# A recurrent attention block and a squared-ReLU FFN: inverting the first round in blocks of 32 steps, later rounds four batches at once, with GpSimd issuing its own loads

## The chip, the cores and the metric

The kernel runs on one core of a Trainium2 chip. The metric is the time of one execution in device microseconds. The core has five engines with an instruction stream each: TensorE (PE in the profile, its weight loads PEld), VectorE (DVE), ScalarE (ACT), GpSimd (POOL) and SyncE (SP), which here only issues transfers. Each engine takes its instructions in the order of the program and waits where data are not there yet.

## The reference

Inputs are r, k, v, w, a, b of shape (4 batches, 8 heads, 768 steps, 40), and the FFN weights w_in (320 x 2048) and w_out (2048 x 320). Each batch and head has a 40 x 40 state:

```
for t in range(S):
    y[t]  = r[t] @ state
    Sa    = state @ a[t]
    state = state * w[t][None, :] - outer(Sa, b[t]) + outer(v[t], k[t])
x   = y rearranged to (B*S, H*D) = (3072, 320)
out = maximum(x @ w_in, 0)**2 @ w_out
```

## The kernel before

The 768 steps are cut into 6 chunks of 128. `order` lists 24 items, chunk by chunk and within a chunk batch by batch: item i has chunk `c = i // 4` and batch `bb = i % 4`. Within a chunk the recurrence becomes matrix products and the inverse of a triangular 128 x 128 matrix per head. That matrix is treated as two diagonal halves of 64 steps (`HC`) and the block N between them.

What is done for an item:

- `early(i)`, wrapped in `prepare(i)`, which first issues the loads of w, b and a for item i + 1 (`load_early`, L133): transposes, running products of the decays and their reciprocals on VectorE (L303 to L312), the 128 x 128 product per head on TensorE, its copy on ScalarE (L319). The triangular parts go to DRAM in `kept_d`, the block N in `kept_n`, decays in `kept_e`. For items 0 and 1 decays and N stay in SBUF. `store` puts each store in `line`, and `tick` issues it on SP's queue a step or two later.
- `solve(u, eng)`, on GpSimd for a unit of items: it loads the triangular halves from `kept_d` into `half_n` (loads issued by SP, L346), and in 63 steps of a product (L352) and a subtraction (L354) makes the inverses in `half_t`, which GpSimd stores to `kept_t` (L356). Units: two batches at once in chunks 0 and 1, four batches in chunks 2 to 5, 8 units in all.
- `inverses(i, g)`: at the first item of a unit it writes out the next unit's solve, then loads item i's N and T (L375, SP).
- `rest(i)`: products with k, r, v and their masks; at its end or in its middle it calls `inverses`.
- `chain(i)`: the dependent part. It needs T and N (L458 to L467; L459 is ScalarE's first copy behind a T product), updates the state and writes the item's tokens.
- `ffn()`: one generator over 12 groups of two items. A group has 24 steps: 16 of w_in products with ReLU and square, and 8 of w_out products.
- `weights(n)`: the weights come as 64-bit floats and are turned into 32-bit ones by five VectorE and two ScalarE instructions per piece (L220 to L230): 12 wide pieces of w_in (512 columns), 16 narrow ones of w_out (320 columns).

The order of the work is written out by hand. `weave` merges several generators step by step into one program order. The head prepares items 0 and 1, solves unit 0, prepares items 2 and 3, does `rest` for items 0 and 1 and rounds 16 pieces beside them. Then for each item i a weave of 12 steps (`TOTAL`) has chain(i), rest(i + 1), one or two prepares, and as many FFN steps as `share` says: (steps in the weave, steps ahead of it), where the steps ahead cover the wait for an inverse. Items 0 to 3 prepare two items each (4 to 11), later ones item i + 8.

All matrix products go through the helper at L78 and all stores of `store` through L99, so these lines appear for many operations; the tile names tell them apart.

Of the kernel before, what the change touches and what calls it, by code (L numbers as in the profile page):

```python
# [8 lines left out]
FP32 = mybir.dt.float32  # L9
I32 = mybir.dt.int32  # L10
U32 = mybir.dt.uint32
Alu = mybir.AluOpType
# [5 lines left out]
def kernel(  # L18
# [22 lines left out]
    nc = tc.nc  # L41
    ctx.enter_context(tc.manual_schedule())
    B, H, S, D = r.shape
    DM = H * D
# [6 lines left out]
    DP = 64  # L51
    NF = DFF // 128
    GB = 2
    LEAD = 2 * B


    NT = NP - 1
# [25 lines left out]
    def new(name, shape, bufs):  # L83
        return work.tile(shape, FP32, tag=name, name=name, bufs=bufs)
# [4 lines left out]
    def later(fn, steps=2):  # L89
        line.append([steps, fn])  # L90

    def tick():
        for entry in line:
            entry[0] -= 1
        while line and line[0][0] <= 0:
            line.pop(0)[1]()

    def store(out_, in_, steps=2):
        later(lambda: nc.sync.dma_start(out=out_, in_=in_), steps)  # L99

    quads = lambda t_: t_.rearrange("p (q t) -> p q t", q=NP)
    by_head = lambda t_: t_[:, :DM].rearrange("t (h d) -> t h d", h=H)
# [20 lines left out]
    def more_rings():  # L123
        for nm in ("k", "b", "r", "v"):
            rings[nm] = Ring(f"in_{nm}", 2, [128, H, DP], 0.0, pads)
# [32 lines left out]
        nc.gpsimd.memset(same[e * DP:(e + 1) * DP, :, e:e + 1], 1.0)  # L158

    more_rings()  # L160
    whole = lambda t_: t_

    UP, DOWN, A_ = range(3)
# [15 lines left out]
    room = w_out.rearrange("p f c -> p (f c)")  # L179
    wide_raws = [room[:, 2 * WI * i:2 * WI * (i + 1)] for i in range(4)]  # L180
    hidden = single("hid", [128, NF + 1, GB * C])
    RAWS = (NF + 1) * GB * C // (2 * DM)
    raws = [hidden.rearrange("p f t -> p (f t)")[:, 2 * DM * i:2 * DM * (i + 1)] for i in range(RAWS)]
    for raw in wide_raws:
        nc.gpsimd.memset(raw, 0.0)
    lowest = single("lowest", [128, 1])
# [13 lines left out]
    def fetch_weights():  # L200
        while count[0] < len(pieces):
            n = count[0]
            wide = n < NARROW
            if len(fetched) + len(begun) >= (4 if wide else RAWS):
                return
            dst, srcs = pieces[n]
            raw = wide_raws[n % 4] if wide else raws[n % RAWS]
            for row, m_, src in srcs:
                nc.scalar.dma_start(out=raw.bitcast(I32)[row:row + m_], in_=src.bitcast(I32))
            fetched.append((dst, raw))  # L210
            count[0] += 1
# [21 lines left out]
    def weights(n, pool=ps_f):  # L233
        for _ in range(n):
# [8 lines left out]
            else:  # L243
# [11 lines left out]

    kept_n = [dram.tile([HC, H, HC], FP32, tag=f"n{i}", name=f"kept_n{i}") for i in range(len(order))]
    Q = HC // 2
    kept_d = [[dram.tile([B, 2, H, Q, HC - n * Q], FP32, tag=f"d{c}{n}", name=f"kept_d{c}{n}") for n in range(2)]
              for c in range(NCH)]
    kept_e = [dram.tile([128, 3, NP, C + 2], FP32, tag=f"e{i}", name=f"kept_e{i}") for i in range(len(order))]  # L260

    units = [(c, b0, 2) for c in range(2) for b0 in range(0, B, 2)] + [(c, 0, B) for c in range(2, NCH)]
    unit_of = {c * B + b0 + n: u for u, (c, b0, nb) in enumerate(units) for n in range(nb)}
    columns = lambda nb: 128 // (nb * 2 * H)
    kept_t = [dram.tile([columns(nb), nb, 2, H, HC // columns(nb), HC], FP32, tag=f"t{u}", name=f"kept_t{u}")
              for u, (_, _, nb) in enumerate(units)]

    def turn(x_):
        p_ = psum(ps_w)
# [19 lines left out]
        return res  # L289

    turned = lambda nm, bufs: new(nm, [128, NP, 128], bufs)

    def early(i, g=None):

# [22 lines left out]
        t_ = new("N", [128, H, C], 1)  # L317
        for e, p_ in enumerate(products(bT, aT[:, :, :C])):
            nc.scalar.copy(t_[:, e * NP:(e + 1) * NP], p_)  # L319
        for n in range(2):  # L320
            for half in range(2):
                at = half * HC + n * Q
                store(kept_d[c][n][bb, half].rearrange("h s t -> s h t"), t_[at:at + Q, :, at:(half + 1) * HC], 1)
        if g is None:
            store(kept_n[i], t_[:HC, :, HC:], 1)
        else:
            g["dec"], g["N"] = dec, new("N21", [HC, H, HC], 2)
            nc.scalar.copy(g["N"], t_[:HC, :, HC:])
        yield

    def solve(u, eng):
        c, b0, nb = units[u]
        cols = columns(nb)
        rows, deep = 128 // cols, HC // cols

        ns = [new("half_n0", [128, Q, HC], 1), new("half_n1", [128, Q, Q], 1)]
        ts = new("half_t", [128, Q, HC], 1)[:, :deep]
        eng.memset(ts, 0.0)  # L340
        flat = ts.rearrange("p j t -> p (j t)")
        for col in range(cols):
            eng.memset(flat[col * rows:(col + 1) * rows, col::HC + cols], -1.0)
        for part, kept in zip(ns, kept_d[c]):
            for col in range(cols):
                nc.sync.dma_start(out=part[col * rows:(col + 1) * rows].rearrange("p s t -> p (s t)"),  # L346
                                  in_=kept[b0:b0 + nb].rearrange("b f h s t -> (b f h) (s t)"))
        yield
        for s in range(HC - 1):
            n, m_ = s // cols + 1, HC - 1 - s  # L350
            p_ = new("half_p", [128, 528], 1)[:, :n * m_].rearrange("p (j t) -> p j t", j=n)
            eng.tensor_tensor(p_, ns[s // Q][:, s % Q, s % Q + 1:].unsqueeze(1).to_broadcast([128, n, m_]),  # L352
                              ts[:, :n, s:s + 1].to_broadcast([128, n, m_]), Alu.mult)
            eng.tensor_tensor(ts[:, :n, s + 1:], ts[:, :n, s + 1:], p_, Alu.subtract)  # L354
            yield
        nc.gpsimd.dma_start(out=kept_t[u].rearrange("two b f h j t -> (two b f h) (j t)"), in_=flat)  # L356
        yield

    def inverses(i, g):
        bb, c = order[i]
        u = unit_of[i]
        if unit_of.get(i - 1) != u and u + 1 < len(units):
            for _ in solve(u + 1, nc.gpsimd):
                pass
        cols, b0 = columns(units[u][2]), units[u][1]
        g["T"] = new("T", [128, H, HC], 2)
        if "N" not in g:  # L370
            g["N"] = new("N21", [HC, H, HC], 2)
            nc.sync.dma_start(out=g["N"], in_=kept_n[i])
        for half in range(2):
            for col in range(cols):
                nc.sync.dma_start(out=g["T"][half * HC + col:(half + 1) * HC:cols],  # L375
                                  in_=kept_t[u][col, bb - b0, half].rearrange("h j t -> j h t"))

    def rest(i, g):
        bb, c = order[i]
# [14 lines left out]
        nc.vector.tensor_tensor(kT, kT_, down[:, :, 1:C + 1], Alu.mult)  # L394
        nc.vector.tensor_copy(ends, down[:, :, 0])
        if unit_of[i - 1 if i else i] == unit_of[i] and i > 1:
            inverses(i, g)
        yield
        g["A"] = masked("A", 4, kT, aT)
        yield  # L400
# [29 lines left out]
            nc.scalar.copy(sd.rearrange("p q e d -> p q (e d)"), quads(p_))  # L430
        yield
        if unit_of[i - 1 if i else i] != unit_of[i]:
            inverses(i, g)
        yield


# [110 lines left out]
    def run(gen):  # L547
        for _ in gen:
            tick()
# [11 lines left out]
            run(gen)  # L561

    def prepare(i, g=None):
        if 1 < i + 1 < len(order) and i + 1 not in early_loaded:
            load_early(i + 1)
        yield from early(i, g)

# [8 lines left out]
    def firsts(begin, end):  # L576
        gens = [prepare(i, ready.get(i)) for i in range(begin, end)]
        next(gens[0]), next(gens[0])
        for i, now in enumerate(gens):
            then = gens[i + 1] if i + 1 < len(gens) else iter(())  # L580
            next(now)
            next(then, None)
            tick()
            yield
            next(now)
            next(then, None)
            tick()
            yield
            run(now)
            yield  # L590

    run(firsts(0, 2))
    while line:
        tick()
    for _ in solve(0, nc.gpsimd):
        pass
    load(0)
    load(1)
    if moe_w_in.dtype != FP32:
        fetch_weights()  # L600

    def head():
        yield from firsts(2, 4)
        yield from rest(0, ready[0])
        yield from rest(1, ready[1])

    WITH = NARROW + 4
    weave((head(), 6 + 2 * 9, 0, WITH + 4), (weights(WITH, ps_c), WITH, 4, WITH + 6))
    while begun:
        rounded_second()  # L610
    while line:
        tick()
    tc.no_sync_barrier()
    inverses(0, ready[0])
    inverses(1, ready[1])
    TOTAL = STEPS // GB

    share = {0: (0, 0), 1: (0, 0), 2: (6, 10), 3: (8, 0), 4: (8, 8), 5: (8, 0)}
    rounding = weights(NF)
    for i in range(len(order)):  # L620
        bb, c = order[i]
        n, ahead = share.get(i, (TOTAL, 0))
        for _ in range(ahead):
            next(second)
            tick()
        tc.no_sync_barrier()
        parts = [(chain(i, ready.pop(i)), 9, 0, TOTAL)]
        if 1 < i + 1 < len(order):
            load(i + 1)
            ready[i + 1] = {}  # L630
            parts.append((rest(i + 1, ready[i + 1]), 9, 2, TOTAL))
        if i < B:
            parts += [(prepare(B + 2 * i), 5, 0, TOTAL - 5), (prepare(B + 2 * i + 1), 5, 5, TOTAL)]
        elif i + LEAD < len(order):
            parts.append((prepare(i + LEAD), 5, 0, TOTAL - 2))
        if i < 2:
            parts.append((some(rounding, 8 - 4 * i), 8 - 4 * i, 0, TOTAL))
        parts.append((some(second, n), n, 0, TOTAL))
        weave(*parts)
    while line:  # L640
        tick()
    run(second)
    while line:
        tick()


# [27 lines left out]
```

## Time and profile before

| what | value |
|---|---|
| three timed runs | 1188.52, 1174.78, 1188.54 us (median 1188.52) |
| the profiled execution: its time / its span | 1178.83 / 1177.1 us |
| mean granted TensorE clock | 0.917 |
| busy: PE / PEld / DVE / ACT / POOL | 999.4 / 829.6 / 491.1 / 233.5 / 731.4 us |
| the two groups of a solve, 504 instructions each (L352, L354) | 333.6 and 366.1 us |
| FFN products: w_in / w_out (matmul time) | 293.1 / 221.0 us |
| ScalarE's L459 copy of items 0, 1, 4, 8, 23 starts at | 131.75, 175.15, 321.9, 525.5, 1107.0 us |

The profile gives one execution. Lines of groups have the source line, engine, operation and tiles, then busy time, the mean time of one in ns, and idle time before it with its cause. Lines of waits give who waited for whom: total, times, longest. Lines of the chain and of timelines begin with the start and the duration in us. Lines of stretches give busy time and count for PE, PEld, DVE, ACT and POOL, then the granted clock (1.00 is full), the share of DMA, and GB/s. Busy time of a matmul includes its pipelined end.

### The profile page before, as it was taken

What the parts mean: (1) busy time and instruction counts of PE and PEld (TensorE: products, weight loads), DVE (VectorE), ACT (ScalarE), POOL (GpSimd) and SP (SyncE); (2) the same over time, 40 slices, a digit from 0 to 9 for tenths busy, and PEclk for the clock granted to TensorE, in tenths of its full rate; (3) what the DMA queues carried; (4) which work ended last, traced back from release to release, by engine and by line L of the source; (5) the groups of instructions that cost most, each with busy time, mean ns of one, the idle gap of its engine ahead of it and who ended that gap; (6) DMA issues with size and microseconds to landing.
All of it is one profiled execution on the core that took longest, in us unless ns stands there. A gap on an engine that the chain in (4) does not pass through costs nothing.

```text
span 1177.1 us, 18561 instructions
## 1 busy us (share of the span) xinstructions
PE 999.4 (85%) x7248; PEld 829.6 (70%) x7248; DVE 491.1 (42%) x1008; ACT 233.5 (20%) x511; POOL 731.4 (62%) x1085
## 2 busy tenths in 40 slices
PE   4232477889999899429999989999989999999998
PEld 3121466778788687318888878788778887888886
DVE  6289576354354155005525424544233242322211
ACT  1033121211221122002112112122122121221211
POOL 4687886488488699979997059994089990000000
PEclk9997556879989899859999989999999999999999
DMA  7946645747655934244663394354353421433000
GB/s 113 169 135 182 137 110 125 146 104 160 152 99 101 170 70 86 48 94 98 109 105 101 86 155 78 87 113 101 92 90 66 77 52 51 76 64 76 3 13 12
DMA packets 261992, 114.95 MB, mean 98 GB/s; under 512 B 243472, under 2 KB 248464, under 8 KB 260368
## 3 DMA queue, kind: packets, MB, share of 16 engines
q1 hardware_dynamic: 256704, 96.98, 43.3%
q10 hardware_dynamic: 4048, 10.49, 3.1%
q0 software_dynamic: 1152, 6.29, 1.4%
q8 instruction: 57, 0.93, 0.4%
q14 instruction: 31, 0.25, 0.1%
HBM read 77.34 MB, written 35.40 MB: 96 GB/s over the span
## 4 chain that ended last, share of the span: by engine, by line
PE 61%; POOL 9%; DVE 5%; DMA 4%; SPq 2%; issue 1%; ACT 0%; POOLq 0%; DVEq 0%; ACTq 0%
PE ps_f L78 34%; PE ps_c L78 16%; PE ps_w L78 6%; POOL half_t L354 5%; POOL half_p L352 4%; PE ps_w L271 4%; DMA dec<-kept_e 2%; DMA T<-kept_t 1%; SPq L133 1%; PE ps_c L428 1%; SPq L99 1%; PE ps_c L471 1%; DVE RV L287 1%; PE ps_w L418 1%; DMA half_n<-kept_d 1%
## 5 line engine op out<-in xcount | busy, mean ns | idle before, releaser
L352 POOL TENSOR_TENSOR half_p<-half_n,half_t 128x252 f32<-128x252 f32 (+52 forms) x504 | 333.6, 662 | 169.6 <-DMA half_n<-kept_d 130.6
L354 POOL TENSOR_TENSOR half_t<-half_t,half_p 128x252 f32<-128x252 f32 (+52 forms) x504 | 366.1, 726 | 39.5
L78 PE MATMUL ps_f<-tokens,w_in 128*128 128x256 f32 x1152 | 293.1, 399 | 0.0
L523 DVE TENSOR_TENSOR hid<-ps_f,hid 128x256 f32<-128x256 f32 x192 | 80.8, 421 | 412.9 <-ACT hid L522 412.8
L78 PEld LDWEIGHTS ps_f<-tokens,w_in 128*128 128x128 f32 x1152 | 216.0, 198 | 31.2 <-issue 0.4
L78 PE MATMUL ps_f<-w_out,hid 128*128 128x320 f32 x768 | 221.0, 437 | 0.0
L78 PEld LDWEIGHTS ps_f<-w_out,hid 128*128 128x128 f32 x768 | 140.7, 190 | 53.9 <-issue 0.2
L522 ACT ACTIVATE hid<-ps_f 128x256 f32<-128x256 f32 x192 | 73.8, 384 | 244.9 <-PE ps_f L78 244.9
L78 PE MATMUL ps_c<-xr,T 64*64 64x40 f32 x768 | 59.4, 239 | 54.1 <-DMA T<-kept_t 52.7
L78 PEld LDWEIGHTS ps_c<-xr,T 64*64 64x64 f32 x768 | 53.7, 147 | 70.3 <-issue 68.2
L78 PEld LDWEIGHTS ps_c<-in_v,A 128*128 128x128 f32 x384 | 50.5, 206 | 17.1 <-DVE w_out L230 14.7
L78 PE MATMUL ps_c<-in_v,A 128*128 128x40 f32 x384 | 49.1, 290 | 14.3 <-DVE w_out L230 14.3
L78 PE MATMUL ps_w<-dec,kvT 40*128 40x128 f32 x384 | 32.4, 316 | 27.3 <-DVE kvT L394 27.2
L78 PEld LDWEIGHTS ps_w<-dec,kvT 40*128 40x128 f32 x384 | 27.3, 215 | 32.2 <-DVE kvT L394 29.2
L78 PE MATMUL ps_w<-decay,bT 40*128 40x128 f32 x352 | 36.8, 340 | 15.4 <-DVE decay L312 13.8
L319 ACT COPY N<-ps_w 128x512 f32<-128x512 f32 x48 | 25.8, 589 | 119.6 <-PE ps_w L78 71.9
L500 DVE TENSOR_TENSOR tokens<-ps_c,dec 128x512 f32<-128x512 f32 x24 | 16.5, 686 | 72.6 <-PE ps_c L78 70.7
L271 PE MATMUL ps_w<-ident,in_w 128*128 128x128 f32 x96 | 19.1, 333 | 32.4 <-DMA in_w<-in_w_dram 31.0
L78 PEld LDWEIGHTS ps_w<-decay,bT 40*128 40x128 f32 x352 | 31.3, 237 | 21.0 <-issue 12.9
L287 DVE TENSOR_TENSOR RX<-ps_w,upper 128x512 f32<-128x512 f32 x48 | 30.8, 682 | 27.0 <-PE ps_w L78 27.0
L78 PEld LDWEIGHTS ps_c<-minus_x,N 64*64 64x64 f32 x384 | 28.1, 153 | 15.3 <-issue 8.5
L307 DVE RECIPROCAL decay<-decay 128x256 f32<-128x256 f32 x22 | 38.3, 1739 | 0.0
(110 smaller groups left out, 1205.8 us busy)
## 6 DMA issues: line engine op xcount, KB each, us to landing
kept_e<-decay SPq DMA_DIRECT2D x22, 780.0 KB
dec<-kept_e SPq DMA_DIRECT2D x22, 780.0 KB
half_n<-kept_d SPq DMA_DIRECT2D x24, 256.0 KB
hid<-in_moe_w_out_dram ACTq DMA_DIRECT2D x16, 320.0 KB
half_n<-kept_d SPq DMA_DIRECT2D x8, 512.0 KB
kept_t<-half_t POOLq DMA_DIRECT2D x4, 1024.0 KB, 5.2
T<-kept_t SPq DMA_DIRECT2D x64, 64.0 KB
in_w<-in_w_dram SPq DMA_DIRECT2D x24, 160.0 KB
```

What stands on the lines that cost most here:

```text
L78: nc.tensor.matmul(o, l_, r_, start=start, stop=True, skip_group_check=True)
L99: later(lambda: nc.sync.dma_start(out=out_, in_=in_), steps)
L133: nc.sync.dma_start(out=t_[:, :, :D], in_=src[bb, :, c * C:(c + 1) * C, :].rearrange("h t d -> t h d"))
L271: nc.tensor.transpose(p_[:, q * 128:(q + 1) * 128], pair(x_, q), ident)
L287: nc.vector.tensor_tensor(t_, p_, over4(upper), Alu.mult)
L307: nc.vector.reciprocal(down[:, :, MID + 1:C + 1], up[:, :, MID + 1:C + 1])
L319: nc.scalar.copy(t_[:, e * NP:(e + 1) * NP], p_)
L352: eng.tensor_tensor(p_, ns[s // Q][:, s % Q, s % Q + 1:].unsqueeze(1).to_broadcast([128, n, m_]), ts[:, :n, s:s + 1].to_broadcast([128, n, ...
L354: eng.tensor_tensor(ts[:, :n, s + 1:], ts[:, :n, s + 1:], p_, Alu.subtract)
L500: nc.vector.tensor_tensor(t_, y_, g["up"][:, :, :C], Alu.mult)
L522: nc.scalar.activation(h_, p_, Act.Relu)
L523: nc.vector.tensor_tensor(h_, p_, h_, Alu.mult)
```

## The change

Chunk 0 is solved in diagonal blocks of 32 steps (Q): 31 steps of GpSimd per solve, still two batches at once. `kept_q` takes these blocks, `kept_m` the 32 x 32 parts that join two blocks of a half (for items 0 and 1 they are copied within SBUF). `inverses` then loads the inverted blocks, transposes them on VectorE, fills T with two ScalarE instructions and makes the joining part with two rounds of 16 small TensorE products, each copied by ScalarE. The tiles for this (`blocks`, `turned`, `mv`, `joins`) lie in slots of `hid`.

From chunk 1 on a unit has four batches: 7 units in all. `solve` is called from the loop once the unit's four items are prepared, and, except for unit 0, GpSimd issues its loads. T comes in two loads per item.

Six rounding pieces stay in the head; 6, 5, 5 and 6 go into the weaves of items 0 to 3. Prepares: 4 and 5 with item 0, 6 and 7 with 1, 8 with 2, 9 with 3, 10 and 11 in a weave ahead of item 4 with 32 FFN steps, then i + 8. FFN steps in the weaves of items 2 to 5: 6, 6, 2, 2. Item 3's early loads stand before `load(0)` and `load(1)`.

```
-    units = [(c, b0, 2) for c in range(2) for b0 in range(0, B, 2)] + [(c, 0, B) for c in range(2, NCH)]
+    units = [(0, b0, 2) for b0 in range(0, B, 2)] + [(c, 0, B) for c in range(1, NCH)]
+    FINE = B // 2
...
     early():
-        for n in range(2):
-            for half in range(2):
-                store(kept_d[c][n][bb, half]..., t_[at:at + Q, :, at:(half + 1) * HC], 1)
+        for half in range(2):
+            for n in range(2):
+                if c == 0:
+                    kept, to = kept_q[bb, :, half, n], at + Q
+                else:
+                    kept, to = kept_d[c][n][bb, :, half], (half + 1) * HC
+                store(kept..., t_[at:at + Q, :, at:to], 1, nc.scalar if g is not None and n else nc.sync)
+            if c == 0 and g is None:
+                store(kept_m[i][half], joins(half), 1)
...
+    def solve(u, queues):
+        fine = u < FINE
+        size = Q if fine else HC
...
+        for part, from_ in zip(parts, kept):
+            for col in range(2):
+                queues[col % len(queues)].dma_start(out=part[col * 64:(col + 1) * 64], in_=from_)
...
+        for s in range(size - 1):
+            n, m_ = s // 2 + 1, size - 1 - s
...
+            nc.gpsimd.tensor_tensor(p_, row..., t3[:, :n, s:s + 1]..., Alu.mult)
+            nc.gpsimd.tensor_tensor(t3[:, :n, s + 1:], t3[:, :n, s + 1:], p_, Alu.subtract)
...
+    def inverses(i, g, queue=nc.sync):
+        if u >= FINE:
+            for col in range(2):
+                queue.dma_start(out=T[col::2], in_=kept[col].rearrange("h f j t -> (f j) h t"))
+        else:
+            blocks = spare("blocks", i)
+            for col in range(2):
+                queue.dma_start(out=blocks[col::2], in_=kept[col]...)
...
+        nc.vector.transpose(upper_..., blocks...)
+        for n in range(2):
+            nc.scalar.activation(T[:, :, n * Q:(n + 1) * Q], blocks, Act.Copy, scale=which[:, n:n + 1])
...
+        for one, two in ends_:
+            for h in range(H):
+                mm(p_[two, 0, h], g["joins"][one, h], upper_[one, h], True)
+        for one, two in ends_:
+            nc.scalar.copy(mv[two], p_[two, 0])
+        yield
+        for one, two in ends_:
+            for h in range(H):
+                mm(p_[one, 1, h], mv[two, h], blocks[two, h], True)
+        for one, two in ends_:
+            nc.scalar.copy(T[one, :, Q:], p_[one, 1])
...
     run(firsts(0, 2))
-    for _ in solve(0, nc.gpsimd):
-        pass
+    flush()
+    solve(0, [nc.sync, nc.scalar])
+    load_early(3)
+    fetch_weights()
     load(0)
     load(1)
     def head():
         yield from firsts(2, 4)
+        flush()
+        solve(1, own)
         yield from rest(0, ready[0])
         yield from rest(1, ready[1])
-    WITH = NARROW + 4
+    WITH = 6
...
-    inverses(0, ready[0])
-    inverses(1, ready[1])
+    for _ in zip(inverses(0, ready[0]), inverses(1, ready[1], nc.scalar)):
+        pass
...
+    ahead = {0: (4, 5), 1: (6, 7), 2: (8,), 3: (9,)}
+    between = {4: (10, 11)}
+    ahead.update({i: (i + 8,) for i in range(4, len(order) - 8)})
-    share = {0: (0, 0), 1: (0, 0), 2: (6, 10), 3: (8, 0), 4: (8, 8), 5: (8, 0)}
+    share = {0: (0, 0), 1: (0, 0), 2: (6, 0), 3: (6, 0), 4: (2, 32), 5: (2, 0)}
+    rounded = {0: NARROW - WITH, 1: 5, 2: 5, 3: 6}
...
+        if before:
+            made = between.get(i, ())
+            jobs = [(some(second, before), before, 0, before)]
+            jobs += [(prepare(m_), 5, 8 * j, 8 * j + 10) for j, m_ in enumerate(made)]
+            weave(*jobs)
...
+        if turn_of < len(order) and all(turn_of + n_ in done for n_ in range(B)):
+            flush()
+            solve(unit_of[turn_of], own)
+            turn_of += B
```

## The prediction

> **What bounds the kernel now.** I read the busy slices first, then the longest waits, the chain that ended last, the queue of SP around the longest wait, and busy time by stretch.
>
> ```profile
> PE   4232477889999899429999989999989999999998
> POOL 4687886488488699979997059994089990000000
> PEclk9997556879989899859999989999999999999999
> ...
> PE ps_c L78 <- DMA T<-kept_t: 52.7, 5, 38.1
> POOL half_p L352 <- DMA half_n<-kept_d: 130.6, 6, 41.2
> ```
>
> A slice is 29.4 us. TensorE is thin in the first eight slices and once more in the middle, at half clock in places; after that it is full. The waits (total, times, longest) say why: 38.1 us at one stroke for an inverse T. The chain that ended last:
>
> ```profile
> 390.13 6.59 DMA half_n<-kept_d
> 462.98 1.53 POOL half_t L354
> 514.49 5.93 DMA kept_t<-half_t
> 521.12 2.28 DMA T<-kept_t
> 523.53 1.91 PE ps_c L78 x16
> ```
>
> Until 523 us GpSimd sets the pace: five solves in a row, four of two batches and one of four. After 523 the chain is TensorE. A late T also holds SP:
>
> ```profile
> 515.01 0.59 SPq L372 DMA_DIRECT2D N<-kept_n  x1
> 520.45 2.60 SPq L375 DMA_DIRECT2D T<-kept_t  x4
> 523.14 0.55 SPq L133 DMA_DIRECT2D in_k<-in_k_dram  x1
> ...
> 525.81 1.09 SPq L133 DMA_DIRECT2D in_w<-in_w_dram  x1
> ```
>
> SP issues in program order: what stands behind the T load leaves after it. The stretches that I price with (PE, PEld, DVE, ACT, POOL busy, clock):
>
> ```profile
> 57.00:120.00 63.00, 20.25 (x122) 17.15 (x122) 57.89 (x104) 22.21 (x40) 51.62 (x91) 0.84 0.56 162
> 131.90:173.30 41.40, 27.91 (x173) 24.42 (x174) 31.47 (x68) 10.67 (x23) 36.89 (x58) 0.54 0.57 115
> 173.30:213.00 39.70, 29.60 (x219) 26.53 (x220) 25.45 (x52) 7.65 (x16) 23.01 (x51) 0.63 0.55 127
> ...
> 523.50:545.00 21.50, 21.22 (x135) 17.89 (x136) 9.32 (x21) 4.37 (x11) 19.19 (x30) 0.76 0.81 121
> 645.70:812.20 166.50, 162.31 (x1233) 134.71 (x1233) 71.63 (x148) 34.02 (x76) 112.34 (x131) 0.97 0.55 105
> 893.10:1107.00 213.90, 213.90 (x1633) 176.33 (x1633) 67.12 (x144) 44.55 (x102) 72.80 (x80) 1.00 0.30 60
> ```
>
> VectorE is 92% busy from 57 to 120 (rounding of weights), TensorE is idle and slow there, and from 645 on it has no room left.
>
> **The change, part by part.** I follow one path: first chain, items 4 to 7 prepared, the solve for chunk 1, item 4, item 8, end.
>
> Solve times. From first product to store, a two-batch solve takes 114.47 - 37.36 = 77.1 us and a four-batch one 514.49 - 396.88 = 117.6. Both have 63 steps; their products have 11,696 and 22,352 elements per partition in all. So a step costs 0.52 us and an element 0.0038 us. A solve of 32-step blocks has 31 steps and 2,856 elements: 16.1 + 10.9 = 27 us. POOL's solves before the steady part go from 4 x 77 + 118 to 2 x 27 + 118.
>
> To the first chain. Solve 0 has two loads of 256 KB in place of eight with 1.5 MB, so I start it at 29 instead of 37 (27 to 33); it ends at 56, its store (512 KB: 3.6 us) lands at 60, the blocks at 63. That is not what ends last: VectorE is. Item 3's loads move ahead of eight others that SP issues at about 1.1 us each, and six of the solve's loads go, so its scans come at 32 and not at 51: 19 us. Of 16 roundings ahead of chain 0 (five instructions each; 3.2 us wide, 2.2 narrow, start to start) six wide ones stay: 6 x 3.2 + 4 x 2.2 = 28 us less. VectorE's last rounding before chain 0 starts at 119.6, so 119.6 - 47 = 73. Then the join, which the trace does not show: the nearest rows for the 128x256 transpose are a 128x256 product of 0.42 us and a reciprocal of 1.74 (near the first: 0.4 each); for 16 small products of two records each, 16 records of 64x40 take 1.1 us at full and 1.9 at half clock, so 2.2 to 3.9 per stage; I take 3. Four stages and ScalarE copies of 0.4 between them: 14 us, to 87, and after A.v (3.6) and its copy ScalarE is at its next rounding at 91; in the trace that is 130.95. GpSimd's second fine solve and own loads lie beside this (done at about 95, wanted past 135): nothing, and without that cover 27 us.
>
> Items 0 and 1. From there to item 1's first L459 copy is 44 us before; six wide roundings for eight narrow ones add 1.6: 137. From it to the N copy of item 7, 175.15 to 213.10, is 38 us; one more rounding (2.9 with its wait) and a fetch that is not begun early (3) make 44: 181, and I give it 165 to 195.
>
> Solve for items 4 to 7. Stores 4 us, GpSimd's own loads 6 (kept_t's 512 KB and 1 MB stores land in 3.6 and 5.2, the four SP loads in 6.6), 117.6, then the store: 309. That takes 6 us to land. Item 4's T load is on SP at the end of item 3, ahead of item 9's five stores and item 11's loads. TensorE by then: items 2 and 3 at 35 us each bring it to 251; the 32 FFN steps ahead of item 4 follow, but item 11's transposes stand after the tenth, so it stops at about 272 and waits for 309 + 6 + 1.3 (two T issues) + 2.5 (five stores) + 3.5 (issue and landing) = 322. The cover holds 22 FFN steps fewer than the listing suggests. Loads that GpSimd issues itself spare SP the four half_n issues of each round, but not this one.
>
> The Trainium skill speaks against that move: "SBUF — State Buffer", section "Who interferes with whom", says that descriptors of a GpSimd DMA starve while VectorE runs in its two-port mode. Here eight kept_t stores issued by GpSimd land in 3.0 to 5.9 us, 4.5 in the middle, with VectorE working beside; by the rule the sum could gain some 2.5 us per load (the page's 3.1 for 0.6), about 1160; by the row it stays.
>
> From 322 to item 8. The trace has the same four chains, rests and prepares with 48 FFN steps from item 11 to item 15: 166.5 us, with a T wait of 3.8. Ahead of item 8 there are 22 + 2 + 2 + 12 + 12 = 50 steps and five prepares. A step is 46.8 / 28 = 1.67 us in the last stretch; an item without a prepare is 213.9 / 6 = 35.65, one with it 40.7, so a prepare is 5. Sum: 166.5 - 3.8 + 5 + 3.3 = 171. Items 4 and 5 have two steps of filler; before, items with six to eight ran 4 to 11 us over their work, so I add 8 each (3 to 14): 187, item 8 at 509. Its solve: item 11's N at 340, 7 for store, 6 for loads, 118, 9 to T: 480. Hidden with 29 us to spare.
>
> From item 8 to the end: 1177.1 - 525.5 = 651.6. T loads no longer stand behind four half_n issues on SP, so the two T waits of 3.8 and the slow clock behind them go: 11 less. 509 + 641 = 1150. The profiled execution took 1178.83 for a span of 1177.1, so 1151.7: **1151 us**. The three timed runs have a median of 1188.52, 9.7 above the profiled one, and a low of 1174.78: the forecast is 0.977 of the profiled run and 0.968 of the median. About 2% can be told from no change.
>
> The trace's restart after the long wait ran at clock 0.76 over 21.5 us with TensorE busy, about 5 us lost, and I leave as much in the stretch after 322. "TensorE: Matmul & The Clock Gate", Part 1, has full rate back after some 3.4 us of work; by it the sum would be about 4 us lower.
>
> **The rivals.**
> No block: if SP were past item 4's T load, or item 11's loads left earlier, all 32 steps would lie under the solve. TensorE would reach chain 4 at about 315 to 318 with 22 steps and a prepare done: 22 x 1.67 + 5 = 42 less, 1109. For it: 32 steps are 53 us, just what is missing. Against: SP at 520.45 above.
> The gain at the head is lost: with four batches at once item 4 waits for item 7's N as well, and for 117.6 instead of 77. If joins and roundings put that N back where it is now, at 213, everything moves by 32: 1183. From 209 on it is slower than the profiled run. For it: VectorE and ScalarE take turns there, 10 of 41 us of VectorE idle; against: 47 us of work and waiting that go.
> A second stall: if item 11's store and the third solve's loads take 29 us longer than I think, item 8 waits. It costs what exceeds 29, so slower than before only from 57 late on. At 75 late it is 1197. For it: POOL waited 41.2 for half_n once; against: SP is free of solve loads.
>
> **How the numbers follow.** Forecast 0.60, with its own range of 1128 to 1172 (N of item 7 from 165 to 195, joins, filler); no block 0.14; head lost 0.18; second stall 0.08. The range 1106 to 1184 takes in the no-block time and leaves out part of the head case and of the second stall. Faster by over 2%: four fifths of the forecast and all of no block, 0.62; within 2%: the rest of it and most of the head case, 0.31; slower by over 2%: 0.07.
>
> **What would show it.** Fine solves of 27 us; first L459 copy near 94; item 7's N near 181; one four-batch solve from 191 to 309; a TensorE gap of about 50 us that ends near 322 in a transpose of in_w and not in a T product; item 8 near 509 with no T wait over 2 us. Wrong if the gap ends in chain 4's T product, if it is under 20 us, or if a second gap stands ahead of item 8.

## The result: 3.6% slower

The changed kernel takes 1226.84 us (median of four runs, 1221.21 to 1230.2); the kernel before took 1185.07 beside it. The ratio is 1.0363, with a 95% interval of 1.0282 to 1.0443. The forecast was 1151. The profiled execution took 1221.21 us for a span of 1219.5.

The same three rows of the busy slices, now 30.5 us each:

```profile
PE   4347677787298989987999978999989999999998
POOL 5670003999517998029996039995059993000000
PEclk9655565788689789997998997999989999999999
```

GpSimd now has long rests (the two fine solves are over by slice 3). TensorE's thin place has shrunk from two slices (4 and 2, the 17th and 18th before) to one (2, the 11th). Yet the span is 42 us longer. The longest waits (total, times, longest) show what took the place of the 38 us for T:

```profile
POOL half_n L376 <- DMA kept_d<-N: 282.5, 5, 100.8
...
DVE kvT L454 <- DMA dec<-kept_e: 48.9, 12, 10.6
...
PE ps_w L281 <- DMA in_w<-in_w_dram: 34.4, 3, 23.2
```

TensorE no longer waits for T. It waits 23.2 us at one stroke for in_w, item 11's first load, and VectorE waits twelve times for `dec`, the decays. GpSimd's 282.5 us are rests between solves and cost nothing. The chain that ended last, around the 23 us:

```profile
323.76 4.20 DMA kept_t<-half_t
327.98 0.66 SPq L401
328.68 0.64 SPq L401
...
332.82 3.35 DMA in_w<-in_w_dram
336.17 0.14 issue
336.30 1.09 PE ps_w L281 x4
```

The solve for items 4 to 7 stores at 323.76; SP, which stood at item 4's T load (L401), goes on at 327.98, and item 11's load is seven issues behind it.

Where the time went, by ScalarE's first copy behind a T product (L459 before, L519 now):

| stretch | before | forecast | after |
|---|---|---|---|
| start to item 0's copy | 131.75 | 94 | 104.15 |
| N of item 7 | 213.10 | 181 | about 189 |
| TensorE's long gap | 485.4 to 523.5 | 272 to 322 | 313.1 to 336.3 |
| start to item 8's copy | 525.5 | 509 | 536.1 |
| from there to the end | 651.6 | 641 | 683.4 |

The head is 24 to 28 us shorter, as meant. It is all gone by item 8, and another 32 us are lost behind it, where I had expected the two kernels to do the same work. They do, but TensorE waits in between. SP's queue as item 8 starts (its T product is at 534.9):

```profile
527.26 1.36 SPq L401 DMA_DIRECT2D T<-kept_t  x2
...
529.40 2.21 SPq L98 DMA_DIRECT2D kept_d<-N  x4
...
535.19 4.62 SPq L132 DMA_DIRECT2D in_b<-in_b_dram  x1
539.85 4.39 SPq L132 DMA_DIRECT2D in_w<-in_w_dram  x1
...
548.18 1.04 SPq L445 DMA_DIRECT2D dec<-kept_e  x1
```

The stores of `kept_d` for the next solve stand behind item 8's T loads. They release GpSimd's own loads of 1.5 MB:

```profile
533.28 2.03 POOL L376 DMA_DIRECT2D half_n<-kept_d  x4 [44.41 <-DMA kept_d<-N]
```

Just then two of SP's loads for the next item need 4.6 and 4.4 us to issue. The decays leave at 548. By stretch (PE, PEld, DVE, ACT, POOL busy, clock, DMA share):

```profile
545.20:554.30 9.10, 0.03 (x2) 0.03 (x2) 0.78 (x3) 0.58 (x1) 8.00 (x15) 0.80 1.11 197
554.30:575.00 20.70, 18.84 (x114) 16.10 (x115) 12.16 (x22) 2.61 (x6) 19.05 (x22) 0.76 0.08 31
```

TensorE stands for 9 us with the DMA engines full, and runs at clock 0.76 in the 20 us behind. The same comes at items 12 and 16 (9.3 and 5.8 us of standing).

### The profile page after: what moved, and what is told of

It reads as the page before. It is cut to its first block, busy times and chain, and to the rows that moved or that the text cites. A ratio compares the mean times of both kernels' runs of the same rounds, so it can differ in the third digit from the quotient of the medians.

```text
span 1219.5 us, 18757 instructions
## 1 busy us (share of the span) xinstructions
PE 1035.6 (85%) x7504; PEld 857.1 (70%) x7504; DVE 491.8 (40%) x1012; ACT 243.5 (20%) x539; POOL 623.5 (51%) x846
## 4 chain that ended last, share of the span: by engine, by line
PE 60%; POOL 9%; DVE 7%; DMA 5%; SPq 3%; issue 1%; ACT 0%; DVEq 0%; ACTq 0%; POOLq 0%
PE ps_f L77 34%; PE ps_c L77 16%; PE ps_w L77 6%; POOL half_t L387 5%; POOL half_p L385 4%; DMA dec<-kept_e 3%; PE ps_w L281 2%; SPq L132 2%; DVE decay L322 1%; DVE decay L323 1%; PE ps_w L478 1%; DVE RV L297 1%; PE ps_c L488 1%; SPq L98 1%; DMA half_n<-kept_d 1%
## 5 line engine op out<-in xcount | busy, mean ns | idle before, releaser
L387 POOL TENSOR_TENSOR half_t<-half_t,half_p 128x62 f32<-128x62 f32 (+26 forms) x377 | 305.6, 811 | 29.5
L385 POOL TENSOR_TENSOR half_p<-half_n,half_t 128x62 f32<-128x62 f32 (+26 forms) x377 | 277.2, 735 | 74.8 <-DMA half_n<-kept_d 29.1
L77 PE MATMUL ps_f<-tokens,w_in 128*128 128x256 f32 x1152 | 300.5, 406 | 6.6 <-DVE w_out L236 5.3
L77 PE MATMUL ps_f<-w_out,hid 128*128 128x320 f32 x768 | 227.6, 445 | 0.0
L376 POOL DMA_DIRECT2D half_n<-kept_d x20 | 10.2, 518 | 282.7 <-DMA kept_d<-N 282.5
L77 PE MATMUL ps_w<-rT,xnT 40*128 40x128 f32 x384 | 36.3, 311 | 21.1 <-DVE RV L297 20.2
L77 PEld LDWEIGHTS ps_w<-rT,xnT 40*128 40x128 f32 x384 | 29.8, 208 | 31.4 <-DVE RV L297 26.0
L297 DVE TENSOR_TENSOR A<-ps_w,upper 128x512 f32<-128x512 f32 x48 | 30.9, 685 | 47.5 <-PE ps_w L77 47.5
L318 DVE TENSOR_TENSOR_SCAN decay<-ps_w,ones 128x64 f32<-128x64 f32 x88 | 23.6, 268 | 60.8 <-PE ps_w L281 60.8
L77 PE MATMUL ps_w<-decay,bT 40*128 40x128 f32 x352 | 29.9, 318 | 18.8 <-DVE decay L327 18.8
```

Source lines behind the costliest of these rows:

```text
L77: nc.tensor.matmul(o, l_, r_, start=start, stop=True, skip_group_check=True)
L297: nc.vector.tensor_tensor(t_, p_, over4(upper), Alu.mult)
L318: nc.vector.tensor_tensor_scan(up[:, q, MID + 1:C + 1], wT[:, q, MID:], ones, 1.0, Alu.mult, Alu.mult)
L385: nc.gpsimd.tensor_tensor(p_, row.unsqueeze(1).to_broadcast([128, n, m_]), t3[:, :n, s:s + 1].to_broadcast([128, n, m_]), Alu.mult)
L387: nc.gpsimd.tensor_tensor(t3[:, :n, s + 1:], t3[:, :n, s + 1:], p_, Alu.subtract)
```

## The experiments

Medians are given with the ratio to the kernel before on the same chip and, in brackets, the 95% interval of the ratio; the changed kernel itself was at 1.0363.

**Who issues the loads.** First the part that the change names.

```
-    own = [nc.gpsimd]
+    own = [nc.sync]
...
-        solve(1, own)
+        solve(1, [nc.gpsimd])
```

> The changed kernel with one part undone: the half_n loads of the solves for chunks 1 to 5 go out by SP again, at the same place in the program. Theory A (GpSimd's own loads run beside SP's loads for the next item and hold them up; TensorE then waits some 9 us for decays near items 8, 12 and 16): those waits fall under 4 us and the time falls by 15 to 30 us, to about 1200. Rival B (it is the 1.5 MB at that moment that costs, whoever issues it): the waits stay within 3 us of 9, 9 and 6 and the time within 8 us of 1227. Rival C (the place behind the stores, with the loads ahead of the next item's on SP, is worse still): over 1235.

1229.6 us, 1.0358 (1.0327 to 1.0389). Behind items 8, 12 and 16 TensorE now stands for in_k (4.6, 4.9 and 5.0 us), with 3.4 us for decays left behind item 12, and once more for 6.5 us behind item 5. Items 9, 13 and 17 follow their forerunner in 48.9, 53.3 and 42.5 us, against 52.1, 53.0 and 42.1 in the changed kernel, so hardly anything is won there and the total stays. Theory A had the waits for decays right and the time wrong. Rival B had the time right, though not the waits: this speaks for the 1.5 MB at that moment, not for the queue. The reverse, GpSimd's loads in the kernel before:

```
-                nc.sync.dma_start(out=part[...]...
+                (nc.sync if u == 0 else nc.gpsimd).dma_start(out=part[...]...
```

> The kernel before with one part of the change done alone: GpSimd issues the half_n loads of all units but the first. Theory A: the loads run beside SP's, waits for decays of 5 to 9 us appear near items 12 and 16, but the two T waits of 3.8 us go and SP is no longer held at its half_n issues; net 0 to 15 us slower, 1185 to 1200. Rival B: no difference beyond 6 us. A reading by the intent of the change (SP is freed): 5 to 15 us faster.

1175.68 us, 0.9914 (0.988 to 0.9948): faster, by as much as the third reading says. By itself this part of the change is a small gain. The two T waits of 3.8 us are gone, and near items 12 and 16 no wait took their place. Behind items 6 and 8 TensorE did stand, 5.3 us for decays and 4.1 for in_k. So loads that GpSimd issues can hold up SP's, but at the old place in the program they mostly don't: theory A fails as the reason for the 42 us.

**When they go.** GpSimd is held until the decays that were late have landed.

```
+    def after_dec(i, g):
...
+        while waiting:
+            nc.gpsimd.tensor_copy(gate, g["up"][:, 0, 0:1])
+            solve(waiting.pop(0), own)
...
```

> The changed kernel with GpSimd waiting, before its own loads for chunks 2 to 5, for the decays of the item after next (a one-column copy that reads them); nothing else moves. Theory A and rival B both want the waits for decays near items 8, 12 and 16 gone (under 2 us each) and 20 to 32 us less, about 1200; the solves start some 20 us later, which their slack before items 8 to 20 should hold. A third reading D (the decays are late by SP's own order, not by the half_n loads): the waits stay and the time is 1227 or more, with T waits added if the slack is too small.

1223.57 us, 1.0304 (1.0273 to 1.0336), a miss in the total and a hit in two of the three places. Item 13's copy follows item 12's by 41.1 us instead of 53.0 and item 17's its forerunner by 33.1 instead of 42.1: 21 us won. Behind item 8 a wait for decays of 3.4 us is left. But the solve for items 8 to 11 had no 20 us to give, and item 8 pays:

```profile
PE ps_c L77 <- DMA T<-kept_t: 17.8, 1, 17.8
```

Reading D is out.

**Why at that moment.** The kernel before loads the same bytes for the same items without such waits, so something else had moved. The diff has it in a line that I had not priced: a single prepare was spread over 10 of the 12 steps of its weave (`TOTAL - 2`) and is spread over 12 now. Its last part, the N copy and the stores of `kept_d`, now comes behind the T loads instead of ahead of them. SP's queue at item 12 in the kernel before:

```profile
671.75 1.83 SPq L99 DMA_DIRECT2D kept_d<-N  x4
...
679.54 2.89 SPq L346 DMA_DIRECT2D half_n<-kept_d  x4
...
683.17 2.59 SPq L375 DMA_DIRECT2D T<-kept_t  x4
687.42 0.40 SPq L133 DMA_DIRECT2D in_k<-in_k_dram  x1
```

There the large loads lead, and the next item's loads leave 8 us after them. The changed kernel with the 10 steps of the kernel before:

```
-            jobs.append((prepare(m_), 5, j * 5, TOTAL - 5 * (len(made) - 1 - j)))
+            jobs.append((prepare(m_), 5, j * 5, TOTAL - 2 if i >= B else TOTAL - 5 * (len(made) - 1 - j)))
```

> The changed kernel with the prepares of items 12 to 23 spread over 10 of the 12 steps of their weave, as in the kernel before, and not over 12. Theory E (the prepare now ends in the last step, so the stores of kept_d and with them the next solve's half_n loads fall behind item 8's, 12's and 16's T loads onto the next item's loads; they ended before them in the kernel before): items 9, 13 and 17 follow their forerunner in 48, 40 and 34 us instead of 52, 53 and 42, and 20 to 32 us go, to about 1200. Rival F (the units' layout in DRAM or GpSimd's queue make the difference, not the place): within 6 us of 1227.

1198.4 us, 1.011 (1.0048 to 1.0172): 28 us gone with two steps. Items 9, 13 and 17 follow in 36.5, 36.4 and 34.8 us, sooner than expected, while items 8, 12 and 16 pay some of it back (52.5, 48.6 and 53.4 us instead of 43.4 each). From item 8's copy to the end it takes 649.9 us instead of 683.4. SP's queue at item 8 in this run, where the stores now lead:

```profile
515.53 1.81 SPq L98 DMA_DIRECT2D kept_d<-N  x4
...
520.46 2.75 SPq L98 DMA_DIRECT2D tokens<-tokens  x4
523.66 1.35 SPq L401 DMA_DIRECT2D T<-kept_t  x2
...
529.06 0.40 SPq L132 DMA_DIRECT2D in_k<-in_k_dram  x1
```

The 1.5 MB now fall on the moves of tokens: TensorE stands 5.0, 4.1 and 4.9 us for these, as it stood 3.8 us for T in the kernel before. Theory E holds, rival F is out. The diff also moves the call of `solve`, from `inverses` ahead of the T loads to the end of the loop; that was not undone by itself.

**The block at SP.** The forecast's own mechanism, tried by letting GpSimd, which waits for its store anyway, issue the T loads of each unit's first item:

```
-                queue.dma_start(out=T[col::2], in_=kept[col]...
+                t_queue.dma_start(out=T[col::2], in_=kept[col]...
...
         if unit_of[i - 1 if i else i] != unit_of[i]:
-            yield from inverses(i, g)
+            yield from inverses(i, g, nc.sync, nc.gpsimd)
```

> The changed kernel with the T loads of the first item of each four-batch unit (items 4, 8, 12, 16, 20) issued by GpSimd behind its own store instead of by SP. Theory of the prediction (SP, held by item 4's T load, keeps back item 11's loads, so that 22 of the 32 FFN steps can't cover the solve): the TensorE gap of 23 us ahead of item 11's transposes goes to under 3 us, item 4 starts near 360 instead of 381, and the time falls by 18 to 23 us, about 1206. Rival: the gap only moves to item 4's T product, since the solve itself is late; then less than 8 us are won.

1198.02 us, 1.0089 (1.0061 to 1.0117). The gap of 23 us is gone, and item 4's copy comes at 353.4 instead of 381.3. By the medians 28 us are won, more than the 18 to 23 expected. GpSimd's timeline shows the T loads behind the store, where they hold back only GpSimd's own next loads:

```profile
324.68 0.60 POOL L390 DMA_DIRECT2D kept_t<-half_t  x1 [0.30 <-POOL half_t L387]
331.28 1.43 POOL L401 DMA_DIRECT2D T<-kept_t  x2 [6.00 <-DMA kept_t<-half_t]
```

Both edits at once:

> Both edits: prepares over 10 steps, and the T loads of each unit's first item issued by GpSimd. If the two losses are separate, they add: about 1227 - 28 - 28 = 1171, 10 to 18 us faster than the kernel before. If they overlap (items 8 to 20 then wait for the solves, whose slack shrinks as TensorE gets ahead): 1180 to 1195, with T waits.

1172.01 us, 0.9873 (0.9814 to 0.9931). The two losses are separate, as far as intervals of some 7 us either way can tell: 28 + 28 is 56, and 55 are won.

**Thin filler.** Twelve of the 32 pieces of `second` that run ahead of item 4's chain move into the weaves of items 4 and 5, six each.

```
-    share = {..., 4: (2, 32), 5: (2, 0)}
+    share = {..., 4: (8, 20), 5: (8, 0)}
```

> The changed kernel with the FFN steps of items 4 and 5 spread as 20 ahead of item 4 and 8 in each of the two weaves, in place of 32, 2 and 2. If two steps of filler are too thin (items 5 and 6 came 32 and 41 us after the item before them), 8 to 14 us less, about 1216; if the chains there are not held by filler, within 4 us of 1227.

1217.95 us, 1.0272 (1.0212 to 1.0331): 9 us under the changed kernel, but the two intervals overlap (1.0282 to 1.0443 there), so the gain is not clear of the noise. Item 8's copy comes at 531.1, so 5 us are won up to there; the rest is not placed.

**The head.**

```
     load(0)
-    load(1)
...
         yield from firsts(2, 4)
         flush()
+        load(1)
```

> The changed kernel with the four loads for item 1 issued after items 2 and 3 are prepared instead of before. Ahead of the first chain ScalarE's N copy of item 3 waits 16 us for item 2's stores, which stand behind eight loads on SP at 2.2 us each. If that wait is what kept the head from being as short as forecast: the first L459-like copy comes 5 to 10 us earlier than 104, N of item 7 as much before 188.6, and the time falls by 4 to 10 us. If VectorE or the rounding loads on ScalarE's queue end last: under 3 us.

1227.23 us, 1.0349 (1.0303 to 1.0395): nothing. The N copy of item 3 comes 3.4 us earlier and the first copy behind T 1.9. ScalarE's timeline in this run:

```profile
23.47 19.33 ACTq L216 DMA_DIRECT2D w_out<-in_moe_w_in_dram  x8
42.89 1.07 ACT L334 COPY N<-ps_w 128x512 f32<-128x512 f32 x2 [20.90 <-DMA w_out<-in_moe_w_in_dram]
52.63 1.07 ACT L334 COPY N<-ps_w 128x512 f32<-128x512 f32 x2 [8.67 <-DMA kept_n<-N]
```

Eight loads of weights for rounding hold ScalarE from 23 to 43, ahead of item 2's N copy. In the changed kernel the same eight took 15.3 us, item 2's N copy came at 38.9, right behind its product, and item 3's at 56.1, after 16.1 us of waiting for item 2's stores. So when item 1's loads leave SP's queue, the weight loads end last in their place. That these weights could leave later was not tried.

**A version that beats both.** The two mended places and the thicker filler:

> Prepares over 10 steps, T of each unit's first item by GpSimd, and the FFN steps of items 4 and 5 as 20 ahead and 8 and 8. The solve's T lands near 331 and item 4's T product stands at 354 there, so 12 steps (20 us) fewer ahead of it should still just cover it. If so, the 9 us that the spread alone brought come on top: about 1163. If the cover is now too short: a T wait ahead of item 4 of 5 us or more, and 1168 to 1175.

1167.78 us, 0.9861 (0.979 to 0.9932): no T wait ahead of item 4, but the 9 us of the spread didn't come on top. Item 4's copy is 15 us earlier than without the spread, item 5's is 3 us later. And with the hold on GpSimd's loads for chunks 3 to 5, whose solves have slack:

> As the last one, with GpSimd's own loads for chunks 3 to 5 held until the decays of the item after next have landed. With prepares over 10 steps these loads fall on the moves of tokens and the T loads, and TensorE waits three times 4 us for tokens. If the 1.5 MB at that moment is the cause, these waits go and 8 to 13 us with them: about 1153. The solves start some 20 us later and have 35 us or more of slack. If tokens wait for SP's order alone: 1163 as before.

1134.68 us, 0.9604 (0.9553 to 0.9656): 4% faster than the kernel before. GpSimd's timeline at item 8:

```profile
506.43 0.18 POOL L701 COPY gate<-dec 128x1 f32<-128x1 f32 x1 [38.47 <-DMA dec<-kept_e]
507.00 2.07 POOL L376 DMA_DIRECT2D half_n<-kept_d  x4 [0.40 <-DMA N<-kept_n]
```

Expected were 8 to 13 us and 33 came. Around item 8 (its copy comes at 515.9 without the hold and at 499.7 with it) the same stretch of both runs says where from, first without the hold and then with it:

```profile
500.00:515.00 15.00, 10.75 (x45) 9.68 (x45) 0.42 (x1) 0.96 (x3) 12.05 (x23) 0.66 1.20 206
```

```profile
500.00:515.00 15.00, 15.00 (x122) 13.14 (x121) 10.06 (x23) 4.42 (x11) 5.11 (x11) 1.00 1.03 212
```

Both move nearly the same bytes in these 15 us (206 and 212 GB/s). Without the hold TensorE has 45 instructions and clock 0.66, with it 122 and 1.00. A standing of 5.2 us cost twice its length: the clock had fallen. Items 8, 12 and 16 now follow in 42.7, 42.7 and 42.3 us (52.8, 48.7 and 53.0 without the hold), which is 27 of the 33 us, and from item 8's copy to the end it takes 635.1 us.

## Why the prediction was wrong

The span was forecast at 1150 and is 1219.5; the 70 us are three terms of the sum.

- **From item 8 to the end, 641 forecast and 683.4 measured: 42 us, the step that failed.** I took this stretch from the kernel before, less 11 us, because its code looked the same, and did not price the two steps by which every prepare from item 12 on ends later. With these two steps undone it took 649.9, so 33.5 of the 42 us are theirs; with the loads held and the thicker filler as well it took 635.1. The 641 were within reach, and the place of five stores in SP's queue was missed. The 11 us that I took off for the T waits show in the kernel before with GpSimd's loads: from item 9's copy to the end it takes 600.5 us there and 610.7 without. None of the rivals had these two steps. The rival nearest to them, a second stall ahead of item 8, did not come: TensorE had no T wait over 2 us.
- **The end of TensorE's gap, 322 and 336.3: 14 us.** The mechanism was right. The gap ended in a transpose of in_w, SP stood at item 4's T load, and the run that took it off won 28 us where "No block" had 42. It is 23 us long and not 50, because from item 7's N to the gap it took about 124 us (189 to 313), with five and six roundings in the weaves of items 2 and 3, and not 91 (181 to 272). Its end is late by 8 us of item 7's N, by 3.5 us of its stores (first issue 7.5 us behind that N, where I had 4), and by GpSimd's own loads: first product 10.5 us after the first issue, where I had 6.
- **From the gap to item 8, 187 and 199.8: 13 us.** Mis-sized, and the cause stays open: the thicker filler was 9 us faster alone, which is not clear of the noise, and brought nothing beside the other edits.

Of the smaller terms the fine solves were right (27.84 to 55.14 is 27.3 us, forecast 27), the join was cheaper (transposes 0.4 us each, all its products in 5.9 us, 12 forecast), and the first copy came 10 us late, at 104.15 for 94. (My own sum gave less than 94: ScalarE's rounding at 91 and the copy 0.8 us behind it, as in the kernel before.) VectorE's last rounding ahead of the first chain comes to its end at 89 and not at 73: it waited 14.6 us, up to 58.4, for ScalarE, whose N copy of item 3 waited for item 2's stores. My sum had that wait at nothing.

The rule of "SBUF — State Buffer", section "Who interferes with whom", against loads issued by GpSimd did not decide the time here: with SP as the issuer the time was the same within the interval (1.0358 and 1.0363), and in the kernel before GpSimd's loads were 0.9% faster. The loads themselves did take longer: from first issue to first product 9.6 to 11.0 us in the five four-batch solves of the changed kernel, and 7.4 to 8.7 with SP as the issuer. Whether starving descriptors are the reason no run here shows.

## What to carry to other kernels

When a diff rewrites a schedule, list for each queue which instructions change places, also those whose step only slides within its slot; a store that releases a large load decides when that load collides. Beside a saturated TensorE, hold large prefetches until the small loads of the next stage have landed, as long as their consumer has slack. A load that waits for another engine's result is better on that engine's queue than at the head of a queue that everybody uses; here that was worth 28 us.

## What the runs showed of the hardware

Three waits of TensorE of 4 to 5 us cost about twice their length. In the run with the thicker filler and no hold it stood 5.18, 4.39 and 4.56 us ahead of items 8, 12 and 16, 14.1 in all, and these items followed 10.1, 6.0 and 10.7 us later than with the hold. The standing of 4.56 us, which began at 834.6, was followed by this:

```profile
838.00:852.00 14.00, 12.84 (x53) 11.20 (x54) 0.85 (x2) 1.56 (x4) 12.31 (x22) 0.50 0.74 148
```

The granted clock is 0.50 over 14 us with TensorE busy for 12.84 of them. "TensorE: Matmul & The Clock Gate", Part 1, has the clock fall after a gap of some 3.4 us, which agrees, and come back after some 3.4 us of work, which these 14 us (and the 21.5 us at 0.76 in the kernel before) do not show. At item 12 it did come back so soon: 0.50 from 671 to 674 and 0.93 from 674 to 676, with the work starting at 671.5. What decides between the two no run here shows.

While 1.5 MB of half_n were landing in the changed kernel, single loads of 160 KB took 4.4 to 5.9 us to issue on SP; such loads took 0.4 to 1.4 us at item 12 in the kernel before. It was so whether GpSimd or SP had issued the large ones (5.37 us for in_v in the latter case).
